# Running sums in the memory of the fifth pair's weights, the first eight heads loaded at once, some loads issued by ScalarE

## The chip, the core and the metric

The kernel runs on one core of one Trainium2 chip. A core has five engines that run side by side: TensorE (matmul, PE in the rows; PEld is its weight load), VectorE (DVE), ScalarE (ACT), GpSimd (POOL) and SyncE (SP, which here only issues DMAs). Each engine works through its own list of instructions in order; they wait for one another by semaphores. The metric is the device time of one execution in microseconds (us); less is better.

## What is computed

Causal attention with a bias from running sums, then a two-layer block, then a soft mixture of eight experts:

```python
# attention: B 4, H 8, S 576, D 64
cum = np.cumsum(np.maximum(s, 0.0), axis=-1)
bias = -(cum[:, :, :, None] - cum[:, :, None, :])
scores = np.where(causal, -1e9, scale * q @ k.T + np.minimum(bias, 0.0))
attn = softmax(scores); x = attn @ v                    # 2304 tokens x 512
# first block: w_in 512 x 2048, w_out 2048 x 512
h = x @ w_in; x = (h * sigmoid(1.702 * h)) @ w_out
# mixture: w_gate 512 x 8, w1 8 x 512 x 1024, w2 8 x 1024 x 512
P = balanced(exp(x @ w_gate))                           # 8 rounds of row and column sums
out = sum(P[:, e:e+1] * (np.maximum(x @ w1[e], 0) @ w2[e]) for e in range(8))
```

The weights of the first block arrive as 64-bit numbers and are turned into two 32-bit parts (a high and a low one) on the chip.

## The kernel before

**Stages.** The program is one long stream. Attention and the first block overlap and take the first 550 us; the mixture of experts, whose matmuls are named `A` to `D`, fills the rest. The change is in the first part.

**Heads and units.** Attention runs in 64 steps here called heads: for each of the four batches the first 256 queries of eight heads (`kend` 256), then the other 320 queries of the same eight heads. Head 0 to 7 (`n < H`) are the short steps of batch 0. Their scores are one plain 32-bit matmul each on a tile `kf` of 66 rows: 64 rows of q and k, and two rows from `aux0` that carry the running sums (`sp<-kf`). From head 8 on, q and k come into a tile `kq`, are split into a high part `one` and a low part `two` (a cast and two subtractions), and four rows of `two` are filled from `aux_d`, a copy of the sums in DRAM, and 64 rows of it by a DMA from `one`. A head's scores (`sp`) go to VectorE (mask, row maximum), to ScalarE (exp), back to TensorE (transposes `tp`), to ScalarE as `pf` or `ph`, to TensorE (`op`, the product with v) and to VectorE (division, into `xg`). When eight heads are done, `xg` is transposed (`xtp`) into `xh` and `xl`, the input of the first block.

**The first block's weights.** They stand in eight pairs of 256 columns, four chunks to a pair, 32 chunks in all. `conv` turns a chunk: two ScalarE passes over `st`, a VectorE pass into `t`, and a cast and a subtraction into `wih`/`wil` or `woh`/`wol` (`split`; the cast goes to VectorE or ScalarE by load). A pair's first matmuls are `hp` (24 matmuls to a token block and pair), its second are `acc` or `accx` (24 too). `NP0 = 4` pairs have memory from the start. Pairs 4 to 6 get theirs when the attention tiles in `spool` are no longer needed (`su.close()` in `convert`), the last pair later.

**The sums.** `sums` computes the first 256 columns of the running sums into `cum` and from there `aux0`; `sums_left`, called after the third unit is scored, does the other 320 columns and writes `aux` and its copy `aux_d`. `aux0`, `aux` and `cum` lie in `auxpool`, which is closed when head 8's `kq` is first wanted (`place_of`); `load_more` doesn't load head 8 before three units are scored and `auxpool` has no work left.

**What sets the order.** Nothing is reordered on the chip. At build time a planner (`Sequencer`) plays the program through with a cost for each instruction: TensorE's instructions are written down when the loop at the end of the kernel finds their inputs ready by that reckoning, and the other engines' instructions are held back and written down in order of readiness and rank (1 goes ahead of 2; conversions of weights have rank 2). So a changed cost or a changed readiness moves hundreds of instructions. What a DMA issue costs stands in `submit` and `issue`.

**DMA semaphores.** In the built program the DMAs of SP and ScalarE take eight semaphores in turn, `DMAHW0` to `DMAHW7`, in the order in which the planner wrote them down. A DMA whose semaphore is still in use by the DMA eight places ahead is issued only when that one has landed; the planner doesn't reckon with this wait.

Of the kernel before, what the change touches and what calls it, by code (L numbers as in the profile page):

```python
# [9 lines left out]
F32 = mybir.dt.float32  # L10
F32R = mybir.dt.float32r
# [46 lines left out]
class Sequencer:  # L58
# [96 lines left out]
    def submit(self, engine, what, call, outs, ins, adds=False):  # L155
# [5 lines left out]
        if what == "dma_start":  # L161
            op.cost = 60 if engine == "SP" else 1000
            op.nbytes = self.size(outs[0]) * outs[0].shape[0] * (2 if self.fine and outs[0].dtype == F16 else 4)
            if adds and self.fine:
                op.nbytes *= ADDING
        else:
            sums = len(outs) > 1
            if engine == "PE":
                op.load = 110 if BYTES[ins[0].dtype] == 4 else 27
            op.cost = self.cost(engine, what, outs[0], ins, sums)  # L170
            op.tail = {"DVE": 85, "ACT": 110}.get(engine, 0) + 90 * sums
# [31 lines left out]
    def issue(self, op):  # L203
# [9 lines left out]
        if op.nbytes:  # L213
            self.issued = max(self.issued, start) + 475
            self.dma = max(self.dma, self.issued + 1200) + op.nbytes / 360
            op.end = self.dma + 440 + op.late
# [119 lines left out]
def kernel(  # L336
# [42 lines left out]
    NP0, NP1 = 4, 7  # L379
# [13 lines left out]
    alloc_w(wpool, range(NP0))  # L393
# [11 lines left out]
    su_aux = ExitStack()  # L405
    auxpool = Pool(seq, su_aux.enter_context(tc.tile_pool(name="auxpool", bufs=1, side=left, reuse_waits="tile")))
    aux0 = auxpool.tile([BH, 4, 256], F32, name="aux0")
    aux = auxpool.tile([2 * BH, 4, S], F32, name="aux")
    cum = auxpool.tile([2 * BH, 2, S], F32, name="cum")
# [166 lines left out]
    spool2 = []  # L576

    def place_of(n):
        if n < H:
            return spool  # L580
        if n >= 2 * H:
            return apool
        if not spool2:
            su_aux.close()
            spool2.append(Pool(seq, su.enter_context(
                tc.tile_pool(name="spool2", bufs=1, side=left, reuse_waits="tile")
            ), aux.tensor.name))
        return spool2[0]

# [12 lines left out]
    def load_qk(n):  # L602
        if n >= len(heads):
            return
        b, h, q0, nq, kend, _, _ = extent(n)
        if n < H:
            kq = spool.tile([66, kend + nq], F32, tag="kq", name="kf", bufs=N_KF)
            nc.sync.dma_start(out=split_qk(kq[0:64], q0), in_=of_qk(qk[b, h, 0:64], n))
            nc.sync.dma_start(out=kq[64:66], in_=aux0[b * H + h:b * H + h + 1])
            qk_of[n] = (kq,)  # L610
            return
        kq = place_of(n).tile([128, kend + nq], F32, tag="kq", name="kq", bufs=3 if n < 2 * H else 1)
        nc.sync.dma_start(out=split_qk(kq, q0), in_=of_qk(qk[b, h], n))
        kq_of[n] = kq
# [18 lines left out]
    def load_more():  # L633
        nonlocal n_qk
        while n_qk < min(len(heads), n_scored + 1 + N_KF if n_qk < H else n_prep + (3 if n_qk < 2 * H else 1)):
            if n_qk == H and (n_s < 3 or auxpool.held()):
                return
# [311 lines left out]
    def do_score():  # L949
# [13 lines left out]
        if n_s == 3:  # L963
            sums_left()
# [185 lines left out]
    def convert():  # L1150
# [12 lines left out]
        if c == 4 * NP0 and stage[0] is spool:  # L1163
            if n_s < NU and units[n_s][0] < 2 * H - 2 or n_v < NU and units[n_v][0] < 2 * H - 2:
                return
            if min(n_pv, n_prep) < 2 * H or spool.held() or spool2[0].held():
                return
# [8 lines left out]
        if c == 4 * NP1 and NP1 not in wih:  # L1176
# [5 lines left out]
            )), range(NP1, NPAIR))  # L1182
        seq.rank = 2
# [670 lines left out]
    sums(0, 256)  # L1854
    for n_qk in range(1, 3):
        load_qk(n_qk - 1)
# [53 lines left out]
    def first_moe():  # L1910
# [3 lines left out]
        def can(j):  # L1914
            p = at_pair[j]
            if p == NPAIR or 4 * p + 2 > n_conv:
# [3 lines left out]
                seq.settled(wih[p].tensor.name), seq.settled(wil[p].tensor.name),  # L1920
            )

        def second(i):
            def when():
# [3 lines left out]
                t = max(seq.settled(x.tensor.name) for x in (gh, gl, woh[p], wol[p]))  # L1928
# [352 lines left out]
```

## Time and profile before

| | us |
|---|---|
| median of 3 runs (2004.87 to 2005.23) | 2005.07 |
| the profiled execution | 2004.55 |
| its span, first to last instruction | 2002.8 |
| TensorE busy | 1963.7 |
| VectorE busy | 1472.6 |
| ScalarE busy | 1252.9 |

How to read it: TensorE is busy in 98% of the span, and idle for 39 us. Some 25 us of these lie in the first 230 us; the 1773 us after that hold 1759 us of TensorE work. A busy TensorE isn't always at full speed: its clock has two levels (1.2 and 2.4 GHz), and the lower one is also found in the first 230 us. A table by stretch, the beginning of the program and its longest gaps stand below, ahead of the prediction.

### The profile page before, as it was taken

The page shows a single profiled execution, that of the slowest core. Times are in us where ns is not written, and L with a number is a line of the kernel's source. Part 1 is how long each engine was busy: PE and PEld are TensorE (multiplying, and loading weights), DVE is VectorE, ACT ScalarE, POOL GpSimd, SP SyncE. Part 2 cuts the span into 40 slices and gives each one's busy share as a digit, 9 for nine tenths or more (in the row PEclk, how much of TensorE's full clock was granted, in tenths as well). Part 3 has the DMA queues.
Part 4 walks back from the last instruction along what each step waited for, and adds up shares of the span by engine and source line. Part 5 has one row for each costly group of instructions (what it writes and reads, how often), then busy time and mean ns, then how long its engine had stood idle before and what let it go on. Part 6 is the DMA issues. An engine that isn't in the chain of part 4 may idle for free.

```text
span 2002.8 us, 40907 instructions
## 1 busy us (share of the span) xinstructions
PE 1963.7 (98%) x15683; PEld 1581.9 (79%) x15683; DVE 1472.6 (74%) x3416; ACT 1252.9 (63%) x2581; POOL 87.5 (4%) x144
## 2 busy tenths in 40 slices
PE   7999999999999999999999999999999999999999
PEld 6889999999988677777777777777777777777777
DVE  5887799887753676988877766776786876777656
ACT  5887677666644575666666666656666666665333
POOL 0000000000000000000000111111101001111000
PEclk9989999999999999999999999999999999999999
DMA  7455345444226454475475566767557556666331
GB/s 222 157 187 172 115 141 171 133 119 123 75 69 213 156 197 151 158 257 182 156 256 144 132 183 176 182 170 204 161 129 245 151 150 185 165 171 182 119 129 43
DMA packets 230100, 322.11 MB, mean 161 GB/s; under 512 B 38272, under 2 KB 156224, under 8 KB 229904
## 3 DMA queue, kind: packets, MB, share of 16 engines
q1 hardware_dynamic: 216944, 295.90, 45.2%
q0 software_dynamic: 12960, 23.60, 8.3%
q8 instruction: 123, 2.02, 0.4%
q14 instruction: 73, 0.60, 0.1%
HBM read 230.85 MB, written 84.34 MB: 157 GB/s over the span
## 4 chain that ended last, share of the span: by engine, by line
PE 81%; DVE 9%; ACT 6%; DMA 3%; issue 1%; SPq 0%; POOL 0%; ACTq 0%; DVEq 0%; POOLq 0%
PE C L294 16%; PE A L294 16%; PE D L294 16%; PE hp L294 8%; PE B L294 8%; PE acc L294 5%; PE sp L294 3%; PE op L294 3%; PE tp L294 2%; ACT h L294 2%; PE accw L294 2%; DVE h L294 2%; DVE hst L294 1%; DMA kq<-in_qk_dram 1%; PE accx L294 1%
## 5 line engine op out<-in xcount | busy, mean ns | idle before, releaser
L294 PEld LDWEIGHTS <-h 128*128 128x128 f16 x6048 | 591.4, 98 | 85.6 <-issue 6.9
L294 PEld LDWEIGHTS <-w1o 128*128 128x128 f16 x4036 | 394.6, 98 | 255.1 <-issue 4.4
L294 PE MATMUL C<-xt,w1o 128*128 128x384 f16 x1152 | 218.6, 326 | 1.4 <-DVE hst L294 1.4
L294 PE MATMUL D<-xt,w1o 128*128 128x384 f16 x1152 | 218.4, 326 | 0.0
L294 PE MATMUL D<-w2o,h 128*128 128x256 f16 x1728 | 217.7, 273 | 0.2 <-ACT y L294 0.2
L294 PE MATMUL A<-xt,w1o 128*128 128x384 f16 x1152 | 214.8, 326 | 0.1
L294 PE MATMUL A<-w2o,h 128*128 128x256 f16 x1728 | 212.2, 273 | 1.8 <-ACT B L294 1.6
L294 PE MATMUL C<-w2o,h 128*128 128x256 f16 x1728 | 208.4, 273 | 1.8 <-DVE y L294 1.7
L294 DVE SCALAR_TENSOR_TENSOR h<-hst,h 128x768 f16<-128x768 f32 (+1 forms) x192 | 138.7, 751 | 56.0 <-ACT h L294 56.0
L294 ACT COPY C<-B 128x384 f32<-128x384 f32 (+1 forms) x168 | 71.5, 426 | 153.6 <-PE B L294 92.6
L294 PE MATMUL hp<-xh,wih 128*128 128x256 f32 (+1 forms) x512 | 156.3, 305 | 0.5 <-DVE t L294 0.5
L294 PE MATMUL hp<-xl,wih 128*128 128x256 f32 (+1 forms) x512 | 154.0, 301 | 0.0
L294 PE MATMUL hp<-xh,wil 128*128 128x256 f32 (+1 forms) x512 | 153.3, 299 | 0.0
L294 POOL DMA_DIRECT2D acc_d<-y x90 | 78.0, 867 | 1219.6 <-DVE y L294 660.3
L294 ACT ACTIVATE h<-hst 128x768 f16<-128x768 f32 (+1 forms) x192 | 126.2, 678 | 3.8 <-DVE hst L294 3.7
L294 ACT ACTIVATE sm<-sm,stats 64x576 f32<-64x576 f32 (+4 forms) x160 | 93.0, 601 | 41.6 <-DVE stats L294 41.2
L294 PE MATMUL acc<-gh,woh 128*128 128x256 f32 x384 | 111.1, 289 | 0.0
L294 PE MATMUL B<-w2o,h 128*128 128x256 f16 x864 | 110.5, 273 | 0.1
L294 PE MATMUL B<-xt,w1o 128*128 128x384 f16 x576 | 109.3, 326 | 0.0
L294 PE MATMUL acc<-gl,woh 128*128 128x256 f32 x384 | 108.5, 282 | 0.0
L294 PE MATMUL acc<-gh,wol 128*128 128x256 f32 x384 | 108.3, 282 | 0.0
L294 ACT COPY B<-A 128x384 f32<-128x384 f32 (+1 forms) x168 | 70.3, 426 | 57.9 <-PE A L294 57.2
(235 smaller groups left out, 3880.3 us busy)
## 6 DMA issues: line engine op xcount, KB each, us to landing
xt<-xc_d SPq DMA_DIRECT2D x168, 384.0 KB
wm<-in_moe_w_dram SPq DMA_DIRECT2D x112, 256.0 KB
w2o<-w_d SPq DMA_DIRECT2D x56, 512.0 KB
wr<-in_moe_w_dram SPq DMA_DIRECT2D x112, 256.0 KB
w_d<-wo SPq DMA_DIRECT2D x98, 256.0 KB
acc_d<-y POOLq DMA_DIRECT2D x90, 256.0 KB, 5.0
kq<-in_qk_dram SPq DMA_DIRECT2D x32, 448.0 KB
st<-in_moe_w_in_dram SPq DMA_DIRECT2D x16, 512.0 KB
```

The source lines that it names most:

```text
L294: self.seq.submit(self.name, what, lambda: method(*args, **named), outs, ins, "accum_op" in named)
```

## The change

Four things are changed together.

- `cum`, `aux` and `aux0` no longer have a pool of their own. They are slices of `auxw`, a tile in the weights' pool that later becomes `wlast`, the memory of the fifth pair's weights. `NP0` is 5: 20 chunks can be turned before the attention tiles are given up. `settled` is asked with a slice where four weights now share one tile.
- `sums_left` is called at the start of the program, ahead of the loads.
- Heads 0 to 7 get eight tiles (two each in the places of `gh`, `gl`, `t` and in `spool`) instead of four in turn, so `load_more` asks for all of them at once. ScalarE issues the loads of heads 2 to 7 and the `aux0` rows of the odd heads; SP issues the others. From head 8 on, `kq` has two buffers instead of three.
- The planner's cost of a DMA issue is 450 on SP (60 before) and 600 on ScalarE in this part, and DMAs no longer wait 475 for one another there beside it.

```diff
         if what == "dma_start":
-            op.cost = 60 if engine == "SP" else 1000
+            op.cost = 1000 if engine == "POOL" else 600 if engine == "ACT" else 60 if self.fine else 450
...
-            self.issued = max(self.issued, start) + 475
+            self.issued = max(self.issued, start) + 475 if self.fine else start + op.cost
...
-    NP0, NP1 = 4, 7
+    NP0, NP1 = 5, 7
...
-    alloc_w(wpool, range(NP0))
+    alloc_w(wpool, range(NP0 - 1))
+    auxw = wpool.tile([128, 32 * 128], F32, tag="last", name="auxw")
...
-    aux0 = auxpool.tile([BH, 4, 256], F32, name="aux0")
-    aux = auxpool.tile([2 * BH, 4, S], F32, name="aux")
-    cum = auxpool.tile([2 * BH, 2, S], F32, name="cum")
+    aux0 = auxw[2 * BH:3 * BH, 0:1024].rearrange("p (r s) -> p r s", r=4)
+    aux = auxw[0:2 * BH, 0:4 * S].rearrange("p (r s) -> p r s", r=4)
+    cum = auxw[0:2 * BH, 4 * S:6 * S].rearrange("p (t s) -> p t s", t=2)
...
         if n < H:
-            kq = spool.tile([66, kend + nq], F32, tag="kq", name="kf", bufs=N_KF)
-            nc.sync.dma_start(out=split_qk(kq[0:64], q0), in_=of_qk(qk[b, h, 0:64], n))
-            nc.sync.dma_start(out=kq[64:66], in_=aux0[b * H + h:b * H + h + 1])
+            tag = ("gh", "gl", "t", "kf")[n // 2]
+            kq = (spool if tag == "kf" else mpool).tile([128, kend + nq], F32, tag=tag, name="kf", bufs=2)[0:66]
+            ask = nc.scalar if n > 1 else nc.sync
+            ask.dma_start(out=split_qk(kq[0:64], q0), in_=of_qk(qk[b, h, 0:64], n))
+            ask = nc.scalar if n % 2 else nc.sync
+            ask.dma_start(out=kq[64:66], in_=aux0[b * H + h:b * H + h + 1])
...
-        kq = place_of(n).tile([128, kend + nq], F32, tag="kq", name="kq", bufs=3 if n < 2 * H else 1)
+        if n < 2 * H:
+            kq = spool.tile([128, kend + nq], F32, tag="kq", name="kq", bufs=2)
+        else:
+            kq = apool.tile([128, kend + nq], F32, tag="kq", name="kq", bufs=1)
...
-        while n_qk < min(len(heads), n_scored + 1 + N_KF if n_qk < H else n_prep + (3 if n_qk < 2 * H else 1)):
-            if n_qk == H and (n_s < 3 or auxpool.held()):
+        while n_qk < min(len(heads), H if n_qk < H else n_prep + (2 if n_qk < 2 * H else 1)):
+            if n_qk == H and n_s < 2:
                 return
...
-        if n_s == 3:
-            sums_left()
...
+        if c == 4 * (NP0 - 1):
+            last = wpool.tile([128, 32 * 128], F32R, tag="last", name="wlast")
...
     seq.holding = True
     sums(0, 256)
+    sums_left()
```

The program's instructions are the same in number and kind, but for a handful of casts that change between VectorE and ScalarE, and for the ten DMAs that change from SP to ScalarE. What moves is shown at three places.

ScalarE at the start of the program, before. `kf` are the tiles of heads 0 to 7, `sm` the scores after the mask; names in brackets are what an instruction waits for.

```order
L294 ACT_TABLE_LOAD
L294 COPY stats_124<-stats_124 128x1 [waits Pool_49]
L294 ACTIVATE sm_231<-sm_231,stats_124 128x128 [waits DVE_49]
L294 ACTIVATE sm_231<-sm_231,stats_124 128x256 [waits DVE_49]
L294 ACTIVATE sm_244<-sm_244,stats_124 128x128 [waits DVE_49]
```

And now:

```order
L294 COPY stats_119<-stats_119 128x1 [waits Pool_49]
L294 DMA kf_206<-in_qk_dram 64x2x256 [waits DMAHW1_49]
L294 DMA kf_207<-in_qk_dram 64x2x256 [waits DMAHW3_49]
L294 DMA kf_208<-in_qk_dram 64x2x256 [waits DMAHW4_49]
L294 DMA kf_209<-in_qk_dram 64x2x256 [waits DMAHW5_49]
L294 DMA kf_210<-in_qk_dram 64x2x256 [waits DMAHW6_49]
L294 DMA kf_211<-in_qk_dram 64x2x256 [waits DMAHW7_49]
L294 DMA kf_205<-auxw_88 2x1x512 [waits DMAHW1_49,DVE_49]
L294 DMA kf_207<-auxw_88 2x1x512 [waits DMAHW2_49]
L294 DMA kf_209<-auxw_88 2x1x512 [waits DMAHW3_49]
L294 DMA kf_211<-auxw_88 2x1x512 [waits DMAHW4_49]
L294 ACTIVATE sm_249<-sm_249,stats_119 128x128 [waits DVE_49]
```

Ten DMA issues stand ahead of the first exp, and each waits for a DMA of eight places before it: `kf_204` is head 0, so the load of head 5 (`kf_209`) waits on `DMAHW5`, which `kf_204<-auxw` uses, and the rows of head 3 (`kf_207<-auxw`) wait on `DMAHW2`, which the first `aux_d<-auxw` uses.

VectorE at the start, before; `cum` are the running sums, the ISA rows are the mask and maximum of the first scores.

```order
L294 TENSOR_SCALAR cum<-cum 64x256
L294 SCALAR_TENSOR_TENSOR cum<-cum 64x256
L294 COPY aux_106<-cum 32x512
L294 ISA sm,stats<-sp,mask 128x128
L294 ISA stats 128x1
```

And now:

```order
L294 TENSOR_SCALAR auxw<-auxw 64x256
L294 TENSOR_SCALAR auxw<-auxw 64x320
L294 SCALAR_TENSOR_TENSOR auxw<-auxw 64x256
L294 COPY auxw<-auxw 32x512
L294 TENSOR_TENSOR auxw<-auxw 64x1
L294 SCALAR_TENSOR_TENSOR auxw<-auxw 64x320
L294 TENSOR_SCALAR auxw<-auxw 32x576 x2
L294 SCALAR_TENSOR_TENSOR auxw<-auxw 32x576 x2
L294 ISA sm,stats<-sp,mask 128x128
```

The sums of the other 320 columns, which stood among the first heads' scores, now stand ahead of them, one of their steps ahead of the copy for which the first scores wait.

TensorE after the last `op` of the first eight heads, before. `vtp` and `vbp` belong to the scale of v, `xtp` are the transposes of the first eight heads' result, `one` and `two` are head 8.

```order
L294 MATMUL vtp<-ident,vmax 2x128
L294 MATMUL xtp<-ident,xg 128x128 x8
L294 MATMUL vbp<-vd,ones_b 128x4
L294 MATMUL sp<-one_112 128x384
L294 MATMUL sp<-two_113 128x384
L294 MATMUL sp<-one_112 128x512
L294 MATMUL sp<-two_113 128x512
L294 MATMUL hp<-xh,wih_72 128x256
```

And now:

```order
L294 MATMUL sp<-one_107 128x384
L294 MATMUL sp<-two_108 128x384
L294 MATMUL sp<-one_107 128x512
L294 MATMUL sp<-two_108 128x512
L294 MATMUL vtp<-ident,vmax 2x128
L294 MATMUL sp<-one_107 64x288
L294 MATMUL sp<-two_108 64x288
L294 MATMUL xtp<-ident,xg 128x128 x4
L294 MATMUL sp<-one_107 64x288
L294 MATMUL sp<-two_108 64x288
L294 MATMUL xtp<-ident,xg 128x128 x4
L294 MATMUL vbp<-vd,ones_b 128x4
```

Head 8's scores move ahead of `vtp`, `xtp` and `vbp`; the first `hp`, which followed head 8's first scores, now comes after all of head 9's. By the order of VectorE, 7 chunks of weights were turned when head 8 was scored, 9 at head 9, 16 at head 16 and 31 at head 24; now it is 0, 3, 9 and 29. At head 27 both have turned all 32 and have 420 `hp` and 384 `acc` matmuls behind them, and from there to the end the lists are nearly the same.

## Rows read from the trace of the kernel before

**Rows 1.** Stretches: from:to, length, busy PE, PEld, DVE, ACT, POOL, clock, DMA, GB/s.

```profile
0.00:35.80 35.80, 26.41 (x104) 23.27 (x104) 17.28 (x68) 18.04 (x37) 4.95 (x23) 1.00 0.81 233
35.80:59.70 23.90, 20.29 (x131) 18.30 (x132) 20.87 (x53) 18.56 (x33) 0.15 (x1) 1.00 0.62 200
59.70:110.40 50.70, 46.34 (x381) 40.31 (x380) 42.09 (x132) 38.80 (x69) 0.90 (x6) 0.93 0.41 123
110.40:168.00 57.60, 52.90 (x498) 51.94 (x496) 53.18 (x152) 51.17 (x109) 0.15 (x1) 0.94 0.64 203
168.00:229.40 61.40, 58.94 (x513) 56.10 (x511) 40.59 (x109) 38.79 (x73) 0.44 (x3) 0.94 0.47 144
229.40:2002.80 1773.40, 1758.80 (x14066) 1392.00 (x14063) 1298.59 (x2905) 1087.52 (x2262) 80.91 (x110) 1.00 0.54 159
```

**Rows 2.** Timeline: start, length in us, engine, line, operation, count, [idle before <-releaser].

```profile
5.06 0.52 DVE L294 COPY aux<-cum 32x512 f32<-32x512 f32 x1
...
5.73 2.62 SPq L294 DMA_DIRECT2D kf<-aux  x4
...
8.67 4.18 PE L294 MATMUL sp<-kf 66*128 66x128 f32 x12 [8.67 <-DMA kf<-aux]
...
10.78 0.85 ACT L294 ACTIVATE sm<-sm,stats 128x128 f32<-128x128 f32 x2 [7.66 <-DVE stats L294]
...
12.16 0.31 DVE L294 TENSOR_SCALAR cum<-cum 64x320 f32<-64x320 f32 x1
...
13.51 0.81 DVE L294 TENSOR_TENSOR_SCAN cum<-cum 64x320 f32<-64x320 f32 x1
...
15.24 0.93 DVE L294 TENSOR_SCALAR aux<-cum 32x576 fp32r<-32x576 f32 x2
...
16.20 1.53 DVE L294 SCALAR_TENSOR_TENSOR aux<-cum,aux 32x576 fp32r<-32x576 f32 x2
...
19.05 1.33 SPq L294 DMA_DIRECT2D aux_d<-aux  x2
...
25.09 0.29 SPq L294 DMA_DIRECT2D two<-aux_d  x1
```

**Rows 3.** SP's own waits, 0 to 60 us: us in total, times, longest.

```profile
SPq L294 <- DMA aux_d<-aux: 0.5, 1, 0.5
```

**Rows 4.** The chain that ended last, 0 to 120 us: start, length, engine, instruction.

```profile
12.84 0.64 PE tp L294 x3
...
44.12 4.79 PE hp L294 x24
...
52.19 2.92 PE hp L294 x24
...
81.04 0.33 PE tp L294 x3
```

**Rows 5.** Timeline of TensorE, its longest gaps after the start, in brackets.

```profile
37.46 0.37 PE L294 MATMUL vtp<-ident,vmax 128*2 128x128 f32 x1 [1.67 <-DVE stats L294]
...
41.75 0.58 PE L294 MATMUL vbp<-vd,ones_b 2*128 2x4 f32 x2 [1.68 <-DVE xl L294]
...
118.41 0.36 PE L294 MATMUL sp<-two 68*128 68x256 f32 x1 [2.46 <-DMA two<-one]
...
123.28 0.88 PE L294 MATMUL tp<-ident,sm 128*128 128x128 f32 x3 [2.25 <-DVE stats L294]
```

**Rows 6.** Stretches at the lower clock, columns as in rows 1.

```profile
99.20:106.00 6.80, 6.34 (x46) 6.04 (x47) 5.97 (x18) 2.44 (x5) 0.17 (x1) 0.50 0.15 42
...
170.90:177.70 6.80, 6.34 (x37) 5.79 (x38) 4.95 (x11) 5.02 (x10) 0.14 (x1) 0.50 0.35 105
```

**Rows 7.** VectorE's groups by form, 35.8 to 110.4 us: busy us, mean ns, idle before.

```profile
L294 DVE SCALAR_TENSOR_TENSOR t<-st 128x512 int32<-128x512 int32 x13 | 8.8, 686 | 0.3 <-ACT st L294 0.2
...
L294 DVE TENSOR_TENSOR wol<-t,woh 128x512 fp32r<-128x512 f32 x8 | 5.5, 684 | 0.1
...
L294 DVE TENSOR_TENSOR gl<-t,gh 128x512 fp32r<-128x512 f32 x3 | 2.0, 677 | 0.0
```

More of the change, by code (lines that the diff above doesn't have):

```diff
@@ L399 @@
     ps_a = Pool(seq, pa.enter_context(tc.tile_pool(name="ps_a", bufs=1, space=PSUM, reuse_waits="tile")))
-    su_aux = ExitStack()
-    auxpool = Pool(seq, su_aux.enter_context(tc.tile_pool(name="auxpool", bufs=1, side=left, reuse_waits="tile")))
-    aux0 = auxpool.tile([BH, 4, 256], F32, name="aux0")
-    aux = auxpool.tile([2 * BH, 4, S], F32, name="aux")
-    cum = auxpool.tile([2 * BH, 2, S], F32, name="cum")
+    aux0 = auxw[2 * BH:3 * BH, 0:1024].rearrange("p (r s) -> p r s", r=4)
+    aux = auxw[0:2 * BH, 0:4 * S].rearrange("p (r s) -> p r s", r=4)
+    cum = auxw[0:2 * BH, 4 * S:6 * S].rearrange("p (t s) -> p t s", t=2)
     nc.sync.dma_start(out=cum[:, 0], in_=s)
@@ L574, in extent @@
         return (g // 2, h, 256, 320, 576, 5, (2, 3, 4)) if g % 2 else (g // 2, h, 0, 256, 256, 2, (0, 1))
[L576 to L588, printed above, removed]
     kq_of, va_of, v3_of, qk_of, outs, live, xgs = {}, {}, {}, {}, {}, {}, {}
@@ L1165, in convert @@
                 return
-            if min(n_pv, n_prep) < 2 * H or spool.held() or spool2[0].held():
+            if min(n_pv, n_prep) < 2 * H or spool.held():
                 return
@@ L1182, in convert @@
             )), range(NP1, NPAIR))
+        if c == 4 * (NP0 - 1):
+            last = wpool.tile([128, 32 * 128], F32R, tag="last", name="wlast")
+            wih[NP0 - 1], wil[NP0 - 1] = (
+                last[:, k * 1024:k * 1024 + 1024].rearrange("p (c f) -> p c f", c=KC) for k in range(2)
+            )
+            woh[NP0 - 1], wol[NP0 - 1] = (
+                last[:, k * 1024:k * 1024 + 1024].rearrange("p (i d) -> p i d", i=2) for k in range(2, 4)
+            )
         seq.rank = 2
@@ L1919, in can @@
                 whole(j) if at_pair[j] == 0 else 0, seq.slot(ps_m, "h"),
-                seq.settled(wih[p].tensor.name), seq.settled(wil[p].tensor.name),
+                seq.settled(wih[p].tensor.name, wih[p]), seq.settled(wil[p].tensor.name, wil[p]),
             )
@@ L1927, in when @@
                     return never
-                t = max(seq.settled(x.tensor.name) for x in (gh, gl, woh[p], wol[p]))
+                t = max(seq.settled(x.tensor.name, x) for x in (gh, gl, woh[p], wol[p]))
                 if p == 0 and i == 0:
```

## The prediction

> **What bounds the kernel now.** I read the busy time by stretch first [rows 1]. From 229.4 us on, TensorE has 1758.8 us of work in 1773.4 us, and the change leaves its list there nearly as it was: nothing is to be won or lost there. The first 229.4 us hold 24.5 us of TensorE idle time. I cut them at five points that can be found again in the changed kernel: the last `op` of the first eight heads (35.8), the last scores of head 9 (59.7), of head 16 (110.4), of head 24 (168.0) and of head 27 (229.4). At head 27 both kernels have all 32 chunks turned and equally many `hp` and `acc` matmuls done, so the change is worth what it does to the moment at which head 27 is reached.
>
> Second, the start of the timeline [rows 2]. TensorE waits 8.67 us for the `aux0` rows of head 0, and then never for a load of the first eight heads. Third, the clock. In the first 48 us the clock column reads 1.00, but the durations say the lower level (1.2 GHz): three transposes take 0.64 us at 12.84 and 0.33 at 81.04, and 24 `hp` take 4.79 us at 44.12 and 2.92 at 52.19 [rows 4]. I go by the durations: TensorE was busy nearly all the time from 8.7 to 35.8 and stayed at the lower level; it rose only after head 8 and the first 24 `hp`. It fell again at 99.2 and 170.9 [rows 6], after gaps. Last, the gaps: 1.67 and 1.68 us with small ones between 35.8 and 42.3, 2.46 and 2.25 at 116 to 123 [rows 5].
>
> **Stretch A, to the last op of the first eight heads (35.8 before).** One step of 0.31 us now stands ahead of the copy into `aux0` [rows 2], which is followed by the DMA of head 0's rows. That DMA took 8.67 - 5.73 = 2.94 us from issue to the first score. So head 0 is scored at 9.0 instead of 8.67.
>
> Head 1's rows are now ScalarE's. Ahead of them in its list are six loads, which wait for semaphores: head 5's load for head 0's rows (9.0), heads 6 and 7's for those of heads 2 and 4, which SP issues 0.65 and 1.3 us after head 0's (2.62 us for four). The last of the six is issued at 10.3, at 0.65 us an issue; head 1's rows then at 10.9. They land at 10.9 + 2.94 = 13.85. Before, three heads were scored in one go of 4.18 us, 1.39 each; now head 1 and 2 follow at 13.85 and are done at 16.6. The first transposes stood at 12.84 [rows 4], so they come 3.8 us later. They also need the first exp. ScalarE gets to it after head 3's rows, which wait for the first `aux_d` copy. On VectorE that needs the steps of 0.81, 0.93 and half of 1.53 us after the `aux0` copy: issue at 8.7. It lands after 2.94 us by the row above, or after up to 6.0 by the copy in the old place, issued at 19.05 and still waited for shortly before 25.09 [rows 2, 3]. With three more issues the first exp falls at 13.5 to 16.6 (before 10.78). The low end is hidden by the wait for head 1; the high end adds 0.8. The old trace has no DMA issued by ScalarE; SP's 0.65 us is the nearest row.
>
> Behind that the stretch is TensorE's own: 26.41 us of work with 0.7 to 0.8 idle, part of which goes, since no conversions stand between the scores on VectorE. A: 3.8 - 0.8 = +3.0, with bounds 0 (the semaphores are free in time) and +5.
>
> One rule of the Trainium skill speaks against this part. The rows show SP's issues at 0.65 us and TensorE never late for the loads of heads 4 to 7 [rows 2]. The page "DMA: Bandwidth & Descriptors", section "Issuing engines are not separate DMA queues", says that DMAs started from several engines run on the same DMA engines and that starting them elsewhere saves only the issuing time. The trace agrees as far as it goes; by the rule the ten moved DMAs bring nothing to the path, which is also what the sum has.
>
> **Stretch B, to head 9 (23.9 us before).** Here 48 `hp` and 12 `acc` go away to later stretches: 4.79 + 2.92 + 12 x 0.122 = 9.2 us. Heads 8 and 9 are prepared during stretch A, so the idle 3.6 us of 35.8 to 42.3 need not come again: there VectorE did divisions, a conversion and the splitting one after the other. But VectorE's new list has, ahead of what frees the bank for head 8's transposes, four masks, the scale of v, a conversion and two `xl`, and ScalarE has seven passes over `st` ahead of head 8's exp; I keep 3.1 us of gap, between 0 and 3.6. B: -9.2 - 3.6 + 3.1 = -9.7, bounds -13 and -9.
>
> **Stretch C, to head 16 (50.7 us).** Nearly the same work as before: 48 `hp` again, 12 `acc` fewer (-1.5), 6 chunks against 7. The clock's rise waits for the first `hp`, which now come here: some 6 us of work at the lower level that had the higher, +3. Against that, part of the 4.4 us idle can go, since less is asked of VectorE at the end of the stretch: -2.5. C: -1.0, bounds -5 and +4.
>
> **Stretch D, to head 24 (57.6 us).** Here the postponed work comes back: 20 chunks instead of 15, 8 products instead of 5, 48 `hp` and 12 `acc` more. VectorE: a chunk is 0.686 + 0.684 us, a product 2 x 0.68 [rows 7]; 53.18 + 5 x 1.37 + 3 x 1.36 = 64.1 us. TensorE: 52.90 + 60 x 0.122 = 60.2. So VectorE is the bound: 64.1 us if it has no gaps, 69.4 if it has them as before (57.6 / 53.18). I take 67.0. D: +9.4, bounds +6.5 and +11.8.
>
> **Stretch E, to head 27 (61.4 us).** The same TensorE work; 2.5 us of idle time and 3.2 us lost to the lower level [rows 1, 6] can go or stay. E: -1.0, bounds -5.6 and +1.
>
> **The sum.** +3.0 - 9.7 - 1.0 + 9.4 - 1.0 = +0.7 us against the profiled execution's 2004.55 (span 2002.8 and 1.75 around it), so 2005.25. The median of the runs is 0.5 above that execution; I say 2005.5. What is won at 36 to 42 us was paid for by moving conversions out of a stretch in which VectorE had time (17.28 busy of 35.8) into one in which it has none.
>
> The other two parts cost nothing. The memory of the fifth pair: its chunks can be turned before the attention tiles are given up, but in the new order chunk 20 comes only around head 22, long after that; the memory is not what the chunks wait for. Two `kq` buffers instead of three: a load is issued a whole head ahead still, and some 7 us of a head (50.7 us for seven) hide it; if a load takes longer than that, the cost is a gap like the 2.46 us at 118.41.
>
> **The rivals.** *VectorE closes up: faster.* If VectorE, with a backlog of conversions that depend on nothing else, has no gaps in D (64.1), the gaps and the lower level of E don't come back (-4.6 more) and A costs 1 instead of 3, the sum is 0.7 - 2.9 - 4.6 - 2.0 = -8.8, some 1996.5; with half of it, 2001. For it: VectorE was at 92% in D already. Against it: its waits there came from TensorE and ScalarE, whose lists are as fixed as its own.
>
> *ScalarE is held by its own DMAs: slower.* The price is stretch A's upper end. If the `aux_d` copy takes the 6.0 us of the old trace and the loads of heads 5 to 7 sit in front of head 1's rows in the queues, ScalarE's first exp comes at 16.6 or later, A is +5, and the lists of D, written down for an earlier start, run with the gaps of before (69.4): 0.7 + 2.0 + 2.4 + 1 = +6.1, 2011. It decides from about 5 us between issue and landing of that copy. For it: the queue is full in the first 30 us (DMA share 0.81). Against it: in the new order the large loads are issued later than the copy.
>
> *The early loads do nothing.* TensorE didn't wait for heads 4 to 7, so loading them early changes only what ScalarE does. Then B's gap stays: +0.5 to the sum, within the forecast.
>
> **How the numbers follow.** About 0.2% (4 us) is what a measurement of this kernel can tell from no change. My forecast, no change beyond that, has 0.44; faster 0.30, most of it 1997 to 2001; slower 0.26, most of it 2009 to 2011. The range takes in both until about 2 in 10 are left out: 1997 to 2011. The likeliest case alone is 2001 to 2009.
>
> **What would show it.** In the new trace: TensorE's second head scored at 13 to 14 us behind a wait for the `auxw` rows, the first exp at 13.5 to 16.6, the last `op` of the first eight heads at 37 to 40; no gap of more than 2 us between that and head 8's scores; the 24 first `hp` still at about 0.2 us each; head 16 at about 103 us, head 24 at 165 to 173, VectorE above 93% busy between them; head 27 within 6 us of 229.4. I am wrong if head 1 is scored right behind head 0, if the clock is at its higher level before the first `hp`, if the stretch from head 16 to 24 takes under 64 or over 70 us, or if the time after head 27 is not 1773 us.

## The result, and the profile after

The changed kernel takes 2022.96 us (median; 2016.28 to 2023.39) beside 2004.97 us of the kernel before. The ratio is 1.0082, with a 95% interval of 1.0061 to 1.0103: it is slower by 12 to 21 us. Three of the four times lie between 2022.87 and 2023.39. The profiled execution, one of the three, took 2023.39 us, its span is 2021.7 (before 2002.8).

First the stretches, cut at the same five points as in [rows 1]: last `op` of the first eight heads, last scores of heads 9, 16, 24 and 27. Columns as there.

```profile
0.00:42.40 42.40, 26.81 (x105) 23.30 (x106) 16.40 (x63) 16.42 (x34) 4.96 (x23) 1.00 0.55 164
42.40:59.50 17.10, 13.66 (x57) 11.68 (x57) 13.38 (x42) 9.66 (x17) 0.15 (x1) 1.00 0.47 152
59.50:106.60 47.10, 43.49 (x352) 38.30 (x350) 39.72 (x125) 38.95 (x70) 0.87 (x6) 0.97 0.49 149
106.60:178.00 71.40, 66.63 (x602) 63.23 (x602) 62.96 (x173) 59.13 (x125) 0.14 (x1) 0.92 0.61 191
178.00:235.70 57.70, 57.28 (x523) 54.82 (x522) 42.15 (x114) 38.08 (x73) 0.44 (x3) 1.00 0.49 154
235.70:2021.70 1786.00, 1761.45 (x14053) 1393.59 (x14052) 1299.01 (x2906) 1087.46 (x2264) 80.70 (x110) 1.00 0.53 158
```

| stretch | before | after | difference | predicted (bounds) |
|---|---|---|---|---|
| A, to the last op of the first eight heads | 35.8 | 42.4 | +6.6 | +3.0 (0 to +5) |
| B, to head 9 | 23.9 | 17.1 | -6.8 | -9.7 (-13 to -9) |
| C, to head 16 | 50.7 | 47.1 | -3.6 | -1.0 (-5 to +4) |
| D, to head 24 | 57.6 | 71.4 | +13.8 | +9.4 (+6.5 to +11.8) |
| E, to head 27 | 61.4 | 57.7 | -3.7 | -1.0 (-5.6 to +1) |
| after head 27 | 1773.4 | 1786.0 | +12.6 | 0 |

Two thirds of the 18.9 us lie where the prediction had nothing. B to E are work that was moved: their sum is -0.3 us. What is left is A and the last line.

**The start.** Timeline of the changed kernel, columns as in [rows 2]; ACTq are DMAs that ScalarE issues.

```profile
4.51 6.95 ACTq L294 DMA_DIRECT2D kf<-in_qk_dram  x6
...
6.46 2.64 SPq L294 DMA_DIRECT2D kf<-auxw  x4
...
9.18 1.62 PE L294 MATMUL sp<-kf 66*128 66x128 f32 x4 [9.18 <-DMA kf<-auxw]
...
11.56 3.31 ACTq L294 DMA_DIRECT2D kf<-auxw  x4
...
14.92 0.80 ACT L294 ACTIVATE sm<-sm,stats 128x128 f32<-128x128 f32 x2 [11.67 <-DMA kf<-in_qk_dram]
15.81 2.93 PE L294 MATMUL sp<-kf 66*128 66x128 f32 x8 [5.01 <-DMA kf<-auxw]
```

Head 0 is scored at 9.18, the second head only at 15.81: TensorE waits 5.01 us for rows that ScalarE issued at 11.56, behind six loads. The first exp comes at 14.92 (before 10.78, [rows 2]). TensorE is idle for 15.6 us of stretch A (42.40 - 26.81), before for 9.4: that is 6.2 of the 6.6 us.

**The end of the first block.** The longest gap after the first scores stands nearly 400 us behind head 27. (Only attention ends near 550 us, with the last `op` at 553 us before and 562 now; the first block goes on to the first matmul of the mixture, `A`, at 667.3 and 686.3.) First TensorE's rows around the gap in the changed kernel, then ScalarE's and VectorE's, then ScalarE's and SP's rows at the same place in the kernel before. `t<-hp` is the activation of the first block, `wm` here a pass over the second expert's weights.

```profile
629.48 0.39 PE L294 MATMUL hp<-xh,wil 128*128 128x512 f32 x1
637.08 0.79 PE L294 MATMUL accw<-gh,wlast 128*128 128x512 f32 x1 [7.21 <-DVE gh L294]
```

```profile
619.08 0.60 ACT L294 ACTIVATE t<-hp 128x512 f32<-128x512 f32 x1 [3.46 <-PE hp L294]
...
630.86 0.63 ACT L294 ACTIVATE wm<-wm 128x512 f32<-128x512 f32 x1 [9.81 <-DMA wm<-in_moe_w_dram]
...
635.20 0.58 ACT L294 ACTIVATE t<-hp 128x512 f32<-128x512 f32 x1
```

```profile
635.80 0.69 DVE L294 SCALAR_TENSOR_TENSOR t<-t,hp 128x512 f32<-128x512 f32 x1 [14.02 <-ACT t L294]
```

```profile
621.57 0.60 ACT L294 ACTIVATE t<-hp 128x512 f32<-128x512 f32 x1 [3.47 <-PE hp L294]
...
623.45 0.63 ACT L294 ACTIVATE wm<-wm 128x512 f32<-128x512 f32 x1
...
627.57 0.58 ACT L294 ACTIVATE t<-hp 128x512 f32<-128x512 f32 x1
```

```profile
602.46 3.28 SPq L294 DMA_DIRECT2D xt<-xc_d  x7
605.79 11.56 SPq L294 DMA_DIRECT2D w1o<-w_d  x14
617.75 13.08 SPq L294 DMA_DIRECT2D wm<-in_moe_w_dram  x16
```

ScalarE waits 9.81 us for the second expert's weights, and the next `t` of the first block stands behind the passes over them: VectorE gets it late, `gh` is late, TensorE is idle for 7.21 us. Before, the same passes began at 623.45 without a wait. The SP rows of the changed kernel are:

```profile
610.86 3.20 SPq L294 DMA_DIRECT2D xt<-xc_d  x7
614.10 10.84 SPq L294 DMA_DIRECT2D w1o<-w_d  x14
625.34 12.63 SPq L294 DMA_DIRECT2D wm<-in_moe_w_dram  x16
```

The loads start 8.4 us later than before, like everything around them (TensorE's first `accw` stands at 591.4, before at 582.6). So the loads are not late; ScalarE's passes stand too early: by the order 63 activations `t<-hp` are ahead of the first of these `wm` passes, before 65. The reason is a line that the diff doesn't show:

```python
            if (p, i) == (NP0 - 1, 0):
                p1b.close()
                begin_weights()
```

The last two token blocks go through the pairs from 7 down to 0, two steps of 5.4 us to a pair. `begin_weights` plans the loads of the first expert's weights (`w1o`) and, behind them, the loads of the second's and the passes over them (`wm`); it is called when pair `NP0 - 1` is reached. With `NP0 = 5` that is pair 4, two steps earlier. On the chip SP's loads start after the same matmuls as before (48 `accw` in both kernels), but ScalarE's list was written for the earlier time.

The gap costs more than itself. TensorE's rows, by window: us, busy, granted clock, DMA share, GB/s.

```profile
629.90:637.10 7.20, 0.02 (x1) 0.72 1.08 358
637.10:642.90 5.80, 5.80 (x13) 0.50 0.61 226
642.90:645.90 3.00, 3.00 (x13) 0.92 0.03 8
```

For 5.8 us behind it the clock is at 1.2 GHz, which is 2.9 us of work lost. With the 7.2 us that makes the 10 us by which the distance between the first `accw` and the first matmul of the mixture grew (84.7 to 94.9 us). The other 2.5 us of the table's last line lie between head 27 and the first `accw` (353.2 us before, 355.7 now), in small waits to which no run puts a price.

### The profile page after: what moved, and what is told of

Its sections match the earlier page's. It is cut to its first block, busy times and chain, and to the rows that moved or that the text cites. A ratio compares the mean times of both kernels' runs of the same rounds, so it can differ in the third digit from the quotient of the medians.

```text
span 2021.7 us, 40897 instructions
## 1 busy us (share of the span) xinstructions
PE 1969.3 (97%) x15683; PEld 1584.9 (78%) x15683; DVE 1473.6 (73%) x3418; ACT 1249.7 (62%) x2579; POOL 87.3 (4%) x144
## 4 chain that ended last, share of the span: by engine, by line
PE 70%; DVE 9%; ACT 6%; DMA 4%; issue 1%; SPq 0%; ACTq 0%; DVEq 0%
PE C L294 16%; PE A L294 16%; PE D L294 16%; PE B L294 8%; PE hp L294 5%; PE acc L294 3%; ACT h L294 2%; PE accw L294 2%; DVE h L294 2%; DMA kq<-in_qk_dram 1%; PE sp L294 1%; PE op L294 1%; PE tp L294 1%; DVE hst L294 1%; DVE sa L294 1%
## 5 line engine op out<-in xcount | busy, mean ns | idle before, releaser
L294 PEld LDWEIGHTS <-h 128*128 128x128 f16 x6048 | 591.4, 98 | 85.4 <-issue 6.7
L294 PE MATMUL hp<-xh,wih 128*128 128x256 f32 (+1 forms) x448 | 136.2, 304 | 2.0 <-DVE t L294 2.0
L294 PE MATMUL hp<-xl,wih 128*128 128x256 f32 (+1 forms) x448 | 133.9, 299 | 0.5 <-DVE xl L294 0.5
L294 PE MATMUL hp<-xh,wil 128*128 128x256 f32 (+1 forms) x448 | 133.4, 298 | 0.0
L294 DVE SCALAR_TENSOR_TENSOR t<-t,hp 128x512 f32<-128x512 f32 x72 | 49.1, 682 | 69.5 <-ACT t L294 69.1
L294 ACT ACTIVATE h<-sb 128x768 f16<-128x768 f32 x96 | 80.8, 842 | 27.1 <-DVE sb L294 26.3
L294 PE MATMUL acc<-gh,woh 128*128 128x256 f32 x336 | 96.7, 288 | 0.0
```

The costliest lines, as they stand in the source:

```text
L294: self.seq.submit(self.name, what, lambda: method(*args, **named), outs, ins, "accum_op" in named)
```

## The experiments

TensorE has the same 15,683 matmuls in all these kernels, so two numbers of each page say where a time comes from: the busy time of PE, which can differ only by the clock (and by overlaps), and the span less that, its idle time.

| kernel | ratio to before (95%) | span | PE busy | idle |
|---|---|---|---|---|
| before | | 2002.8 | 1963.7 | 39.1 |
| after | 1.0082 (1.0061 to 1.0103) | 2021.7 | 1969.3 | 52.4 |
| late_by_hand | 1.0029 (1.0016 to 1.0042) | 2012.1 | 1968.9 | 43.2 |
| late_rows_sp | 0.9997 (0.9988 to 1.0007) | 2002.4 | 1964.1 | 38.3 |
| late_sp | 1.0018 (1.0009 to 1.0028) | 2009.8 | 1968.4 | 41.4 |
| before_act | 1.0034 (1.0022 to 1.0046) | 2012.1 | 1964.7 | 47.4 |
| late_oldcost | 1.0007 (0.9998 to 1.0017) | 2003.8 | 1961.9 | 41.9 |
| before_newcost | 0.9997 (0.9988 to 1.0007) | 1998.9 | 1960.6 | 38.3 |
| rows_sp_oldcost | 1.0020 (1.0011 to 1.0030) | 2007.3 | 1964.6 | 42.7 |
| late_sums3 | 1.0087 (1.0072 to 1.0102) | 2019.1 | 1965.8 | 53.3 |
| before_sums | 0.9962 (0.9948 to 0.9976) | 2001.9 | 1965.3 | 36.6 |
| before_sums_again | 0.9973 (0.9963 to 0.9984) | 1996.0 | 1958.5 | 37.5 |
| sums_copy_late | 1.0027 (1.0017 to 1.0036) | 2007.6 | 1968.0 | 39.6 |
| sums_eight_loads | 0.9983 (0.9974 to 0.9992) | 2001.3 | 1964.2 | 37.1 |
| mem_only | 1.0014 (1.0004 to 1.0023) | 2004.9 | 1964.0 | 40.9 |
| sums_kq2 | 0.9994 (0.9984 to 1.0003) | 2001.3 | 1964.0 | 37.3 |
| sums_eight_newcost | 0.9988 (0.9976 to 1.0001) | 2000.2 | 1962.4 | 37.8 |
| sums_newcost | 0.9968 (0.9955 to 0.9982) | 1994.3 | 1959.1 | 35.2 |

### The line that reads NP0

late_by_hand is the changed kernel with

```diff
-            if (p, i) == (NP0 - 1, 0):
+            if (p, i) == (3, 0):
```

> The changed kernel, but the loads of the first expert's weights are planned at the same wide step of the first block as before (pair 3; in the changed kernel NP0, now 5, puts them at pair 4). Nothing else differs; ScalarE's list has 65 activations t<-hp ahead of the first wm pass again, where the changed kernel has 63. Theory (the 7.2 us gap at 629.9 us and the lower clock behind it come from the wm passes that stand two steps too early in ScalarE's list): the gap goes, the first matmul A comes 9 us later than before instead of 19, and the time is 2012.5 to 2013.5. Rival (the loads themselves are late, since the first block is late): the gap stays and the time is 2023.

Measured: 2010.64 us and 1.0029, by the ratios 10.6 us less than the changed kernel and 2 us below what the theory had. Its page shows 43.2 us of idle time instead of 52.4, and the first matmul `A` comes at 676.9, 9.6 us later than before (expected 9). ScalarE at the same place:

```profile
631.13 0.60 ACT L294 ACTIVATE t<-hp 128x512 f32<-128x512 f32 x1 [3.47 <-PE hp L294]
...
633.01 0.63 ACT L294 ACTIVATE wm<-wm 128x512 f32<-128x512 f32 x1
```

The wait of 9.81 us is gone, as the theory said. All further kernels whose names begin with late, as well as rows_sp_oldcost and mem_only, have this line.

### ScalarE's issues

late_rows_sp takes the odd heads' `aux0` rows from ScalarE:

```diff
             ask = nc.scalar if n > 1 else nc.sync
             ask.dma_start(out=split_qk(kq[0:64], q0), in_=of_qk(qk[b, h, 0:64], n))
-            ask = nc.scalar if n % 2 else nc.sync
+            ask = nc.sync
             ask.dma_start(out=kq[64:66], in_=aux0[b * H + h:b * H + h + 1])
```

late_sp has `ask = nc.sync` in the first line as well, so that SP issues the loads too; before_act puts the changed kernel's four lines into the kernel before.

> As late_by_hand, but all aux0 rows are issued by SP; the loads of heads 2 to 7 stay on ScalarE, six issues ahead of its first exp. Conversions as in the changed kernel (0, 4, 9, 29 at heads 8, 9, 16, 24). Theory (the 5.0 us gap behind the first head is the odd heads' rows standing behind six loads in ScalarE's list): the gap is under 1 us, the first exp at 11.5 to 12.5, and the last op of the first eight heads where late_sp had it, 38 to 39 us. Rival (the six loads fill the DMA queues and hold any row): the gap stays at 3 us or more.

> As late_by_hand, and all loads and aux0 rows of the first eight heads are issued by SP, none by ScalarE. The order of conversions is nearly the one of the changed kernel (0, 3, 9 and 29 chunks at heads 8, 9, 16 and 24). Theory (ScalarE's ten issues hold the second head and the first exp): the second head is scored right behind the first, the first exp comes at 11 to 12 us instead of 14.9, the last op of the first eight heads at 36 to 38 instead of 42.4, and the time is 5 us below late_by_hand, 2008. Rival (what is won at the start is lost by head 24, since the postponed conversions set head 24 and 27): the last op is early all the same, head 27 is not, and the time is within 1.5 us of late_by_hand.

> The kernel before, with the loads of heads 2 to 7 and the aux0 rows of odd heads issued by ScalarE, and nothing else; four at a time as before, so ScalarE has four DMA issues ahead of its first exp. By the order 4, 7, 16 and 32 chunks at heads 8, 9, 16 and 24. Theory (ScalarE's issues hold the second head's rows and the first exp): the second head is scored behind a gap of 1.5 to 3 us, the last op of the first eight heads 2 to 4 us later than before, the time 1 to 4 us above before. Rival (the issues on ScalarE are covered): within 1 us of before, with no gap behind the first head.

late_rows_sp is as fast as the kernel before (0.9997): by the ratios the rows on ScalarE cost 6.4 us. ScalarE's six loads, SP's rows, the first scores and the first exp in its timeline, then its stretch A, with the columns of [rows 1]:

```profile
3.64 7.22 ACTq L294 DMA_DIRECT2D kf<-in_qk_dram  x6
...
6.46 3.23 SPq L294 DMA_DIRECT2D kf<-auxw  x5
...
8.75 4.18 PE L294 MATMUL sp<-kf 66*128 66x128 f32 x12 [8.75 <-DMA kf<-auxw]
...
10.91 0.81 ACT L294 ACTIVATE sm<-sm,stats 128x128 f32<-128x128 f32 x2 [7.67 <-DMA kf<-in_qk_dram]
```

```profile
0.00:36.60 36.60, 26.45 (x105) 23.40 (x106) 17.61 (x67) 16.63 (x34) 4.96 (x23) 1.00 0.70 202
```

Three heads in one go again, the exp 4 us earlier, the last `op` at 36.6 where late_by_hand has 42.5, and head 27's last scores still 5.8 us ahead of it. The six loads still take 7.22 us of ScalarE's list, and the DMA engines are busier than in the changed kernel (share 0.70 beside 0.55 in stretch A); so it was not that the six loads hold any row, as the rival had it. Two things went with the rows. ScalarE issued head 1's at 11.56 us, for their place in its list, where SP issues its second row at 7.27. And from issue to score they took 4.25 us, where SP's first row takes 2.29 (6.46 to 8.75). Whether a row takes longer on its way because it follows loads that the same engine issued, no run separates from its place in the list. That the first exp came before the 11.5 us of the expectation, and the last `op` before its 38, makes the effect larger than the theory had it.

In before_act, with two loads ahead of the rows instead of six, the gap is smaller and there all the same, and the kernel is 6.8 us slower than before (expected 1 to 4):

```profile
7.91 1.85 ACTq L294 DMA_DIRECT2D kf<-aux  x2
...
8.09 1.62 PE L294 MATMUL sp<-kf 66*128 66x128 f32 x4 [8.09 <-DMA kf<-in_qk_dram]
12.63 2.90 PE L294 MATMUL sp<-kf 66*128 66x128 f32 x8 [2.92 <-DMA kf<-aux]
```

Here too head 1's rows take long from issue to score, 12.63 - 7.91 = 4.72 us. The gap itself is 2.9 us; the last `op` of the first eight heads comes 5.7 us later than before (expected 2 to 4). The order of the conversions changed as well, and what the rest is made of is not shown.

late_sp lies between (1.0018 beside 1.0029 of late_by_hand; the intervals overlap): 2.2 us below late_by_hand, where its theory had 5 and its rival at most 1.5. There SP issues four more loads ahead of the rows, and the first scores come late:

```profile
7.14 3.23 SPq L294 DMA_DIRECT2D kf<-auxw  x5
...
10.56 4.21 PE L294 MATMUL sp<-kf 66*128 66x128 f32 x12 [10.56 <-DMA kf<-auxw]
```

10.56 beside 8.75: to let ScalarE issue the loads is worth 1.8 us at the start, so long as the rows stay on SP. The rule cited in the prediction (the Trainium skill, "DMA: Bandwidth & Descriptors", section "Issuing engines are not separate DMA queues": another engine saves only the issuing time) covers 0.7 us of it, the rows being issued at 6.46 instead of 7.14. The other 1.1 us is not issuing time: from issue to score SP's first row took 3.42 us behind its own four loads, and 2.29 where ScalarE had issued them.

### The planner's cost of an issue

late_oldcost and rows_sp_oldcost take the two planner lines back, before_newcost puts them into the kernel before.

> As late_by_hand, with the planner's two lines on the cost of a DMA issue as before the change. By the order VectorE then has 5, 9, 20 and 32 chunks turned at heads 8, 9, 16 and 24 (changed kernel: 0, 3, 9, 29; before: 7, 9, 16, 31), and ScalarE has 7 DMA issues ahead of its first exp. Theory (the planner's new issue cost is what moved the conversions out of the first 110 us, and that is where stretch D's 14 us come from): head 24 comes at or before 168, head 27 at 225 to 230, and the time is 2003 to 2008. Rival (the start held by ScalarE's issues decides, whatever stands behind it): head 27 at 234 to 236, the time 2012 to 2013.

> The kernel before, with only the two planner lines on the cost of a DMA issue changed. By the order 7, 10, 16 and 31 chunks are turned at heads 8, 9, 16 and 24, as before. Theory (the new cost postpones conversions only together with the early loads): 2003 to 2008. Rival (the new cost alone brings the 9 us to head 63): 2012 to 2014.

> As late_rows_sp, with the planner's old cost of a DMA issue: 1, 5, 12 and 28 chunks at heads 8, 9, 16 and 24. If the new cost is a loss of its own in the changed kernel (late_oldcost was 4 us below late_by_hand), 1999 to 2001; if late_oldcost gained only because fewer of ScalarE's issues stood ahead of its first exp (7 instead of 10), 2003.5 to 2005, as late_rows_sp.

The old cost makes late_by_hand 4.4 us faster, and late_rows_sp 4.6 us slower; in the kernel before the new cost makes no difference (0.9997). rows_sp_oldcost, at 2008.96 us, fits neither of its theories. The time of late_oldcost was as its theory had it, but not by its way: head 24 came at 179.8 and head 27 at 233.1 (expected 168 and 225 to 230), with 432 `hp` behind it instead of 420. With 7 issues ahead of the first exp instead of 10, its second head is scored at 12.74 behind a gap of 1.95 us (15.81 and 5.01 in the changed kernel); whether that is its gain is not shown. So no price of their own is seen for these lines, faster in one kernel, slower in another, the same in a third. They write another order each time, and which one is better was not to be told from the number of chunks turned early: late_oldcost has 20 at head 16, sums_eight_newcost 5, and the second is the faster.

### The early sums

before_sums is the kernel before with `sums_left()` moved to the start; late_sums3 takes that back in late_by_hand (with the `n_s < 3` of `load_more`); sums_copy_late is before_sums with only the two copies to `aux_d` at the old place.

> The kernel before, with sums_left called at the start as in the changed kernel, and nothing else. By the order this alone postpones the conversions: 2, 4, 9, 15 and 29 chunks at heads 8, 9, 16, 20 and 24 (before 7, 9, 16, 20, 31; changed kernel 0, 3, 9, 16, 29). SP issues all loads. Theory (postponing costs by itself, since TensorE reaches its upper clock only with the first hp and has fewer hp and acc to fill the first 110 us): 3 to 6 us slower than before. Rival (postponing only moves work): within 1.5 us of before.

> The kernel of before_sums once more, for more runs beside those of before and for a second profile: the first profile (2003.62 us) was the slowest of its five runs, the other four took 1996.5 to 1999.3. If early sums alone gain, the ratio is 0.9950 to 0.9975 again; if the first value came from one good chip, it is within 0.001 of 1.

> As late_by_hand, but sums_left is called after the third unit is scored, as before the change. By the order 1, 5, 13, 20 and 30 chunks at heads 8, 9, 16, 20 and 24, ten ScalarE issues ahead of the first exp as in the changed kernel. Theory of before_sums: the time is 2 to 4 us below late_by_hand (2007 to 2009), the first hp at 50 to 56 us. Rival: within 1.5 us of late_by_hand, since the gap of 5 us behind the first head is still there.

> before_sums, but the two copies to aux_d are issued after the third unit, as in the kernel before; VectorE's sums stay at the start. If early sums gain because head 8's rows (two<-aux_d) are there earlier, the gain goes and the time is within 2 us of before; if they gain because VectorE has no sums among the first heads' scores, it stays 4 to 7 us below before.

before_sums postpones the conversions just as the changed kernel does (9 chunks at head 16) and is faster than the kernel before, by 0.9962 and by 0.9973 in the repetition: some 5 to 8 us. The theory that postponed conversions cost by themselves has fallen; sums_eight_newcost below, with 5 chunks at head 16, says the same.

late_sums3 came out 12 us above late_by_hand where 2 to 4 below were expected. Its start looks like the reason:

```profile
5.12 8.54 ACTq L294 DMA_DIRECT2D kf<-in_qk_dram  x5
...
8.49 1.14 SPq L294 DMA_DIRECT2D st<-in_moe_w_in_dram  x2
...
13.76 2.79 ACTq L294 DMA_DIRECT2D kf<-auxw  x3
...
17.60 2.93 PE L294 MATMUL sp<-kf 66*128 66x128 f32 x8 [7.88 <-DMA kf<-auxw]
```

ScalarE needs 8.54 us for five loads. By the order, the load of head 6 waits on the semaphore of the first `st`, a load of 512 KB, that SP issues ahead of it (first SP's instruction, then ScalarE's):

```
L294 DMA st_242<-in_moe_w_in_dram 128x2x512 [waits DMAHW1_49]
L294 DMA kf_210<-in_qk_dram 64x2x256 [waits DMAHW1_49]
```

Without the early sums the places in the rotation of the eight semaphores are others, and what ScalarE waits for is large: the fourth load is issued at 8.96, for 0.54 us, and head 6's only at 13.12, 3.6 us after that. In the changed kernel the same six loads had 3.0 us of waits between them: issued at 4.51, 6.51, 7.77, 9.07, 9.65 and 10.51, 0.5 to 1 us each.

But by itself this isn't the 12 us. The last `op` of the first eight heads comes at 43.4, only 1 us later than in late_by_hand, and up to 100 us the two kernels have the same idle time of TensorE, 21.4 us. At the end late_sums3 has 10.1 us more of it, 7.1 of them from 100 to 240 us. Whether the late start or the later sums make the waits there is open.

sums_copy_late lost the gain, as the first of its theories said, and more: it is some 4 to 5 us slower than before (1.0027), not within 2. Its trace doesn't bear that theory out: head 8's first scores stand at 40.80 us, in before_sums_again at 40.26. Its busy time is 9.5 us longer (1968.0 to 1958.5). By what the early sums gain is left open.

### Memory, early loads, and the best of them

sums_eight_loads is the kernel before with early sums, eight tiles and ScalarE's loads; sums_eight_newcost has the planner's new cost as well; mem_only has the memory part, with the eight tiles and the two `kq` buffers that go with it; sums_kq2 is before_sums with the following line, and the 2 in place of the 3 in `load_more`:

```diff
-        kq = place_of(n).tile([128, kend + nq], F32, tag="kq", name="kq", bufs=3 if n < 2 * H else 1)
+        kq = place_of(n).tile([128, kend + nq], F32, tag="kq", name="kq", bufs=2 if n < 2 * H else 1)
```

> The kernel before with early sums, eight tiles for the first eight heads loaded at once, and ScalarE issuing the loads of heads 2 to 7 (SP all aux0 rows); not changed are the memory of the fifth pair (NP0 = 4, a pool for the sums, three kq buffers) and the planner's costs. By the order 2, 4, 9, 16 and 28 chunks, nearly those of late_rows_sp. If the fifth pair's memory and the new cost are worth nothing either way, 2003.5 to 2005 as late_rows_sp; if early loads are worth nothing and what separates late_rows_sp from before_sums is the memory or the cost, 1996 to 2000.

> The kernel before with the memory part of the change alone: the sums as slices of the tile that becomes wlast, NP0 = 5 (the loads of the first expert kept at their old place), the first eight heads in eight tiles but loaded as far ahead as before, all by SP, two kq buffers; sums_left after the third unit and the old planner costs. By the order 3, 5, 12, 20 and 29 chunks at heads 8, 9, 16, 20 and 24. If the fifth pair's memory with the smaller kq is a loss of its own (rows_sp_oldcost was 7 us above sums_eight_loads), 2009 to 2013; if that was the sum of several lists that happen to differ, within 2 us of before.

> before_sums with two kq buffers instead of three from head 8 on, nothing else. If the third buffer is needed, TensorE waits for loads of kq or two between heads 8 and 16 and the time is 2 to 5 us above before_sums, 2002 to 2005; if a load is always a head ahead (as the prediction had it), 1998 to 2000.

> sums_eight_loads with the planner's new cost of a DMA issue: late_rows_sp without the fifth pair's memory. By the order the conversions come later than in any kernel so far: 0, 1, 5, 14 and 25 chunks at heads 8, 9, 16, 20 and 24. If postponed conversions cost by themselves, 2005 to 2010; if they only move work (as in before_sums), 1999 to 2003.

> before_sums with the planner's new cost of a DMA issue. By the order 1, 2, 10, 16 and 29 chunks at heads 8, 9, 16, 20 and 24. If the gain of the early sums stands by itself, 1996 to 2000, 5 to 9 us below before; if the new cost spoils it (the first hp after head 9 instead of ahead of it), 2003 to 2006.

The early loads and the eight tiles bring nothing beside the early sums (0.9983 and 0.9988 beside 0.9962 and 0.9973). mem_only is 2.8 us slower than before (1.0014): not the 2009 to 2013 of its one theory, and at the edge of the 2 us of the other; before_sums with two buffers for `kq` is 4 us slower than with three (0.9994 beside 0.9973). Neither speaks for the prediction's "cost nothing", but what each part costs is not shown: mem_only holds both, and no row of sums_kq2 shows TensorE waiting for a `kq` load. Its idle time is that of before_sums_again (37.3 and 37.5), the busy time is longer by 5.5 us, and that can be the clock's (last section).

sums_newcost, two of the four parts, beats both kernels: 0.9968, 1998.91 us, with 35.2 us of idle time, the least of all. Against before_sums (0.9962 and 0.9973) it makes no difference that these runs can tell.

## Why the prediction was wrong

The forecast was 2005.5 us and no change, the range 1997 to 2011; it came out at 2022.96. Two steps failed.

**"The change leaves its list there nearly as it was"**, of TensorE after 229.4 us. It was read from TensorE's list, whose matmuls do come in nearly the same order. The table of chunks and `hp` at head 27 agreed too, and still ScalarE's list had six passes two steps earlier. The step missed that `NP0` is read in a line outside the diff. late_by_hand puts a price on it: 10.6 us. Among the signs that it would be wrong by, the prediction had "the time after head 27 is not 1773 us"; it was 1786.0.

**Stretch A, bounded at +5.** The mechanism was right: head 5's load waits for head 0's rows, the odd heads' rows stand behind six loads, the second head waits for them, the first exp falls at 14.92 (13.5 to 16.6 predicted). The term for the rows was too small. The last of the six loads was issued at 10.51 (10.3 predicted), but the rows of head 1 at 11.56 instead of 10.9, their issue took 1.44 us instead of 0.65,

```profile
10.51 0.95 ACTq L294 DMA_DIRECT2D kf<-in_qk_dram  x1
11.56 1.44 ACTq L294 DMA_DIRECT2D kf<-auxw  x1
```

and from issue to the score they took 15.81 - 11.56 = 4.25 us, where the 2.94 of head 0's rows had been taken [rows 2]. So the second head was 2 us later than predicted. The 0.8 us of small gaps that were to go became 1.4 (42.40 - 26.81 - 9.18 - 5.01), and A was +6.6. The upper bound should have held it: the same rows had shown up to 6.0 us for another copy, and that bound was given to the copy alone.

The rest:

- The rival "ScalarE is held by its own DMAs", at 0.26 with its slower part at 2009 to 2011, is what happened, though not by the copy to `aux_d` that it named: it was the rows. With the `NP0` line set right the kernel takes late_by_hand's 2010.6, within its price. That the ten moved DMAs "bring nothing to the path" was wrong of the rows, which cost it 6.4 us. Of the loads late_sp shows 1.8 us gained at the start, sums_eight_loads no gain beside before_sums.
- **Stretch D** was said to be VectorE's (64.1 us of work; 62.96 measured). But TensorE had 66.63 of 71.40 us, 13.7 more than before, where 7.3 had been reckoned for 60 matmuls. There were 104 more: left out of the sum were 36 `op` matmuls (B has 16 fewer and C 8) and 9 transposes `tp`. And there was more work at the lower clock (granted mean 0.92 beside 0.94). TensorE had less idle time there than VectorE, the engine named as the bound, and the 71.4 us passed the 70 that the prediction had named as a sign against it.
- **B and C** were each off by 3 us, in opposite directions, D by 4.4 and E by 2.7, in opposite directions too; the four add up to -0.3 us, where -2.3 had been predicted. That the postponed work comes back was right; that the sum came so near is in part luck.
- The clock was right: it rose only with the first `hp`, which stood at 59.7 us. Before, they began at 43.9.
- That the other two parts cost nothing isn't borne out: mem_only, which has both, is 2.8 us slower than before, and sums_kq2 about 4 us slower than before_sums, though how is open.
- The early sums, which the prediction only charged (0.31 us ahead of head 0's rows), gain 5 to 8 us by themselves. In the changed kernel that gain was given back: late_rows_sp, with both faults mended, is at 0.9997. By which of the other parts is not shown.

## What to carry to other kernels

Before you call the rest of a program unchanged, look for every line that reads a constant the diff changes, and compare every engine's list up to the end, not TensorE's alone: six ScalarE passes two steps too early cost more than all that was moved at the start. A small DMA on which the next step waits must not stand behind large ones in an engine's list, least of all on an engine that also computes: each issue there waits for the semaphore of a DMA eight places back, and in late_sums3 a load of 128 KB waited 3.6 us for one of 512 KB. When one change has four parts, run each alone: here one of them gains 5 to 8 us, and the whole loses 16.

## What was not expected of the hardware

before_sums and before_sums_again are the same program, and their profiled executions differ by 5.9 us in span (2001.9 and 1996.0). The idle time is the same within 1 us (36.6 and 37.5); the busy time isn't (1965.3 and 1958.5). TensorE's windows show where most of it arises: us, busy, granted clock, DMA share, GB/s, first of before_sums, then of before_sums_again.

```profile
44.00:52.00 8.00, 8.00 (x51) 1.00 0.59 196
52.00:60.00 8.00, 7.32 (x56) 0.92 0.49 154
60.00:68.00 8.00, 8.00 (x40) 0.50 0.24 69
68.00:76.00 8.00, 8.00 (x55) 0.73 0.24 69
```

```profile
44.00:52.00 8.00, 8.00 (x60) 1.00 0.57 189
52.00:60.00 8.00, 7.25 (x63) 1.00 0.47 147
60.00:68.00 8.00, 7.98 (x64) 1.00 0.48 138
68.00:76.00 8.00, 7.65 (x67) 1.00 0.53 164
...
92.00:100.00 8.00, 5.92 (x72) 0.84 0.51 144
100.00:108.00 8.00, 8.00 (x62) 0.73 0.57 176
```

Up to 44 us both run alike; by 52 the one has done 9 matmuls fewer in as much busy time. Then its clock is at the lower level for some 13 us, with TensorE busy nearly all the time, and in the other not at all there: the first 300 matmuls took it 6.4 us more of busy time. The other's clock falls later, from 92 to 108 us, for some 7 us, and that gives back only part. The times of this kernel's other runs go from 1996.07 to 2004.11 us, and over all the kernels here the busy time for the same matmuls goes from 1958.5 to 1969.3. A difference of 3 or 4 us between two orders of this kernel can therefore be the clock's, and a profile should be compared by idle time and busy time apart.
